# First tile in written order, with the float64 weights' last bits made by ScalarE

## The chip, the cores and the metric

One core of a Trainium2 chip runs the program. Its engines are TensorE (PE, with its weight loads PEld), VectorE (DVE), ScalarE (ACT), GpSimd (POOL) and SyncE (SP), which issues nearly all DMAs. The metric is the device time of one execution in microseconds, lower is better. An engine works through its instructions in the order in which they stand in its queue; where one waits, everything behind it on that engine waits too.

## The reference

Attention through 32 packed queries per head, then a two-dimensional Fourier transform added to its input, then a normalised two-layer network with a residual. 8 batches, 8 heads, 576 tokens, head size 64, so x has 576 rows of 512 for each batch and 4608 rows in all.

```python
def sm_attn(qq, kk, vv):
    s = scale * np.matmul(qq, kk.transpose(0, 1, 3, 2))
    s = s - np.max(s, axis=-1, keepdims=True)
    a = np.exp(s)
    a = a / (np.sum(a, axis=-1, keepdims=True) + 1e-09)
    return np.matmul(a, vv)
p_packed = sm_attn(p, k, v)
out = sm_attn(q, p_packed, p_packed)
...
X = np.fft.fft(x, axis=1)
X = np.fft.fft(X, axis=2)
mixed = np.real(X).astype(np.float32)
u = x + mixed
mu = np.mean(u, axis=-1, keepdims=True)
var = np.mean((u - mu) ** 2, axis=-1, keepdims=True)
un = (u - mu) / np.sqrt(var + 1e-06)
ch = np.maximum(un @ w_ch1, 0.0) @ w_ch2
return (u + ch).astype(np.float32)
```

The two weight matrices, 512x2048 and 2048x512, come in as float64 and are made float32 on the chip.

## The kernel before

**The work.** The 4608 rows are cut into 36 blocks of 128, and the blocks into nine tiles of four. The network (`ffn`) takes one tile at a time. Its hidden layer of 2048 is cut into 16 chunks j of 128. `up(j)` makes the hidden values of chunk j: 12 matmuls of 128x512 into the PSUM tile `ph`, of which there is one. ACT then takes `hh`, the rounded relu of `ph`, and DVE `hl`, what the rounding left. `down(j)` adds chunk j to the four sums `acc`: 12 matmuls again. Values and weights are split into a rounded part and a rest (`wr_h` by ACT, `wr_l` by POOL, line 107 inside `split`; `uh`, `ul` for the rows), and every product is three matmuls. A pair `wr_h`, `wr_l` is made anew for each chunk, matrix and tile.

**The loop.** For chunk j the program writes: `up(j)`, a split, `step(2j)`, `down(j-1)`, a split, `step(2j+1)`. Each `step` also runs one piece of the front of the next batch, the generator `front(b)`: scores `s`, exponentials, packed values `po`, spectra `pg`, `py`, `pz`, values `px`, and at the end the blocks `ubuf`. In the first tile this is the front of batch 1, and its pieces go by the letters of `ORDER[1]`; a `y` there ends a half step's piece. The letters that matter here: `e0 q1 e1` stand in step 14 and `m0`, `m1`, `a0 a1` in steps 15, 16 and 17 (softmax of the second attention for head groups 0 and 1; POOL makes the three sweeps over `s` for group 0, DVE for group 1). `f0 r0 h0` stand in step 18 and `f1 r1 h1` in step 20: they fold the transposed weights `a` into `eo` and `f` and split `f` into `fh` (ACT) and `fl` (DVE); group 0 is folded by POOL, group 1 by DVE. Still in step 20 come the products `py` and `pyr` of table t = 0 from `fh`, `fl`, `gh`, `gl` of both groups, and in step 21 those of t = 1.

**The order of the queues.** From the second tile on, PE, DVE, ACT and POOL work in the order in which the program is written (`tc.manual_schedule`). In the first tile `nullcontext()` stands there instead: a scheduler sets the order of all queues, by its own costs. SP's order is the scheduler's in all tiles.

**The weights.** The first tile runs while the weights still come in. Chunk (j, n) of matrix n is 512 KB of float64, seen as pairs of 32-bit words. It is fetched into one of the places of the `STG` tables: a negative number is a part of the weights' own final storage that isn't written yet (`w1f`, `w2f`), 9 is a part of `ubuf`, `None` one of the two `wst` tiles. Then it is converted by three instructions of 128x512: `top` (ACT) takes sign, exponent and upper digits from the high word, and `bits` (DVE) shifts that by 3 and puts in the top 3 bits of the low word. Chunks 0 and 1 are done ahead of the tile; `load_weights(j + 2)` does both chunks of j + 2 in every even step, from step 0 to step 26.

Of the kernel before, what the change touches and what calls it, by code (L numbers as in the profile page):

```python
# [1 line left out]

# [1 line left out]

# [76 lines left out]
def tile_kernel(ctx, tc, kpT, qT, v, w1, w2, tabH, tabL, tabR, tabB, tabT, sel, ident_d, out):  # L81
    nc = tc.nc
# [63 lines left out]
    fetched = {}  # L146

    def spot(n, part, shape):

        t = (w1f, w2f)[n].rearrange("p j n -> p (j n)")[:, (part % NJ) * DM:]  # L150
        size = shape[1] * shape[2]
        return t[:, 0:size].rearrange("p (a n) -> p a n", a=shape[1])

    def fetch(j, n):
        i = stages.pop(0)
        if i is None:
            st = work.tile([P, 512, 2], I32, tag="wst", name="wst", bufs=2)
        elif i < 0:
            st = spot(n, i, [P, 512, 2]).bitcast(I32)
        else:  # L160
            st = ubuf[:, i:i + 2, :].rearrange("p a n -> p (a n)").bitcast(I32).rearrange("p (n t) -> p n t", t=2)
        nc.sync.dma_start(st, (w1, w2)[n][:, j, :].bitcast(I32).rearrange("p (n t) -> p n t", t=2))
        fetched[j, n] = st

    def chunk(j, n):
        return (w1f, w2f)[n][:, j, :].bitcast(I32)

    def top(j, n):
        if (j, n) not in fetched:
# [4 lines left out]
        return nc.scalar.activation(c.bitcast(F32), high.bitcast(F32), AF.Prelu, scale=REBIAS, alpha=-2.0 ** 32)

    def bits(j, n):
        low, c = fetched.pop((j, n))[:, :, 0], chunk(j, n)
        nc.vector.tensor_scalar(c, c, 3, None, ALU.logical_shift_left)
        nc.vector.scalar_tensor_tensor(c, low, 29, c, ALU.logical_shift_right, ALU.bitwise_or)  # L179
# [7 lines left out]
    meant = {}  # L190
# [60 lines left out]
    def front(b):  # L251
# [41 lines left out]
        def scores(*gs):  # L293
# [11 lines left out]
            for g in gs:  # L305
# [101 lines left out]
        def less_one(g):  # L407
# [6 lines left out]
            def exps():  # L414
                nc.scalar.activation(s2, s2, AF.Exp, scale=0.125)
                nc.scalar.activation(s2, s2, AF.Copy, bias=-1.0)

# [105 lines left out]
        def folded_parts(g):  # L523
# [10 lines left out]
            def low():  # L534
# [94 lines left out]
        for t, base in enumerate((0, FO) if b else ()):  # L629
# [15 lines left out]
            st = work.tile([P, N2], F32R, tag=f"yr{t}", name="yr", bufs=1)  # L645
# [376 lines left out]
```

## Time and profile before

| | |
|---|---|
| device time, median of 3 | 1011.98 us (1010.78 to 1012.79) |
| the profiled execution | 1009.1 us, of it 1007.3 us span |
| ahead of the first network tile | 0 to about 50 us |
| first tile, from the first `hh` to the sixteenth | 56.5 to 170.7 us |
| second tile, the same | 180.2 to 278.4 us |
| busy over the span | PE 96%, PEld 79%, DVE 61%, POOL 46%, ACT 42% |

PE is the engine that counts: it is busy nearly all the time, so the kernel gets shorter only where PE stops waiting or has less to do. In the first tile PE has waits that the later tiles don't have. Busy time of DVE, ACT or POOL matters there only when PE waits for what they make.

### The profile page before, as it was taken

How to read it: one execution, taken by the hardware profiler on the slowest of the kernel's cores; microseconds unless marked ns; L12 is line 12 of the kernel's file. 1: busy time of each engine (PE TensorE's matmuls, PEld its weight loads, DVE VectorE, ACT ScalarE, POOL GpSimd, SP SyncE). 2: the span in 40 equal slices, each digit the busy share in tenths (PEclk: the TensorE clock that was granted, in tenths of full speed). 3: DMA queues.
4: the chain of work that ended last, by engine and by line, in shares of the span. 5: the costliest groups of instructions: out<-in, count | busy, mean ns of one | idle time of the engine just before them, and what ended most of it. 6: DMA issues, size and time to landing. Idle time of an engine off the chain costs nothing.

```text
span 1007.3 us, 15127 instructions
## 1 busy us (share of the span) xinstructions
PE 971.7 (96%) x5706; PEld 792.3 (79%) x5706; DVE 610.9 (61%) x1215; ACT 424.6 (42%) x882; POOL 465.7 (46%) x413
## 2 busy tenths in 40 slices
PE   6899799999999999999999999999999999999998
PEld 4777587878877887788878887778778888887886
DVE  5888986578555956685657755694658452323112
ACT  3466345444444445343444444443433443233322
POOL 3236625455336434553445435543454354544443
PEclk9999999999999999999999999999999999999999
DMA  9336440310122004300231114110211010111001
GB/s 352 119 110 223 151 126 22 142 50 21 43 95 98 22 1 135 99 21 22 84 102 49 43 42 142 50 63 18 99 48 37 27 63 1 47 38 43 0 1 43
DMA packets 36938, 72.82 MB, mean 72 GB/s; under 512 B 4225, under 2 KB 18433, under 8 KB 36865
## 3 DMA queue, kind: packets, MB, share of 16 engines
q1 hardware_dynamic: 35856, 70.34, 20.6%
q0 software_dynamic: 1008, 1.51, 0.5%
q8 instruction: 45, 0.74, 0.3%
q14 instruction: 29, 0.23, 0.1%
HBM read 55.58 MB, written 16.25 MB: 71 GB/s over the span
## 4 chain that ended last, share of the span: by engine, by line
PE 71%; DVE 13%; issue 7%; POOL 4%; ACT 3%; DMA 1%; ACTq 0%; SPq 0%; POOLq 0%; DVEq 0%
PE ph L789 32%; PE acc L806 27%; POOL wr_l L107 3%; DVE turned L453 1%; DVE turned L447 1%; PE po L350 1%; DVE hl L796 1%; PE s L289 1%; PE px L249 1%; PE px L247 1%; PE px L248 1%; ACT hh L795 1%; PE pz L247 1%; PE e1tp L327 1%; PE py L249 1%
## 5 line engine op out<-in xcount | busy, mean ns | idle before, releaser
L107 POOL TENSOR_TENSOR wr_l<-w1f,wr_h 128x512 fp32r<-128x512 f32 x144 | 189.4, 1317 | 393.7 <-ACT wr_h L104 392.8
L796 DVE SCALAR_TENSOR_TENSOR hl<-ph,hh 128x512 fp32r<-128x512 f32 x144 | 98.6, 685 | 298.9 <-ACT hh L795 298.7
L789 PE MATMUL ph<-uh,wr_h 128*128 128x512 f32 (+1 forms) x580 | 230.1, 397 | 10.5 <-DVE hl L796 6.6
L107 POOL TENSOR_TENSOR wr_l<-w2f,wr_h 128x512 fp32r<-128x512 f32 x144 | 195.9, 1361 | 86.0 <-ACT wr_h L104 80.2
L806 PE MATMUL acc<-wr_l,hh 128*128 128x512 f32 x576 | 225.8, 392 | 5.5 <-POOL wr_l L107 5.5
L789 PE MATMUL ph<-uh,wr_l 128*128 128x512 f32 (+1 forms) x580 | 226.3, 390 | 1.5 <-POOL wr_l L107 1.5
L806 PE MATMUL acc<-wr_h,hh 128*128 128x512 f32 x576 | 226.3, 393 | 1.2 <-ACT wr_h L104 1.2
L789 PE MATMUL ph<-ul,wr_h 128*128 128x512 f32 (+1 forms) x580 | 226.1, 390 | 0.0
L806 PE MATMUL acc<-wr_h,hl 128*128 128x512 f32 x576 | 224.9, 390 | 0.0
L795 ACT ACTIVATE hh<-ph 128x512 fp32r<-128x512 f32 x144 | 86.1, 598 | 325.7 <-PE ph L789 325.7
L789 PEld LDWEIGHTS ph<-uh,wr_h 128*128 128x128 f32 x580 | 109.3, 188 | 47.0 <-issue 15.4
L806 PEld LDWEIGHTS acc<-wr_l,hh 128*128 128x128 f32 x576 | 108.1, 188 | 29.7 <-POOL wr_l L107 9.0
L789 PEld LDWEIGHTS ph<-uh,wr_l 128*128 128x128 f32 x580 | 109.1, 188 | 25.3 <-POOL wr_l L107 2.0
L806 PEld LDWEIGHTS acc<-wr_h,hh 128*128 128x128 f32 x576 | 108.1, 188 | 24.0 <-ACT wr_h L104 2.2
L789 PEld LDWEIGHTS ph<-ul,wr_h 128*128 128x128 f32 x580 | 109.5, 189 | 21.5 <-issue 0.8
L806 PEld LDWEIGHTS acc<-wr_h,hl 128*128 128x128 f32 x576 | 108.2, 188 | 22.8
L104 ACT CAST wr_h<-w2f 128x512 fp32r<-128x512 f32 x144 | 89.4, 621 | 0.0
L104 ACT CAST wr_h<-w1f 128x512 fp32r<-128x512 f32 x144 | 88.4, 614 | 1.5 <-DVE w1f L179 1.3
L223 ACT ACTIVATE junk<-ubuf,stat 128x512 f32<-128x512 f32 x36 | 25.9, 720 | 55.9 <-DVE stat L218 55.9
L107 POOL TENSOR_TENSOR gl<-turned,gh 128x516 fp32r<-128x516 f32 x14 | 21.8, 1555 | 18.7 <-ACT gh L104 18.7
L227 POOL TENSOR_TENSOR stat<-stat,mhalf 128x1 f32<-128x1 f32 x36 | 24.6, 696 | 6.9 <-DVE stat L226 6.9
L453 DVE TENSOR_TENSOR turned<-turned 128x258 f32<-128x258 f32 x32 | 27.5, 898 | 0.5
(207 smaller groups left out, 1283.4 us busy)
## 6 DMA issues: line engine op xcount, KB each, us to landing
kp<-kpT SPq DMA_DIRECT2D x16, 608.0 KB, 5.0
out<-ubuf SPq DMA_DIRECT2D x36, 256.0 KB, 2.1
vt<-v SPq DMA_DIRECT2D x14, 640.0 KB, 4.4
wst<-w SPq DMA_DIRECT2D x17, 512.0 KB, 3.8
qt<-qT SPq DMA_DIRECT2D x14, 576.0 KB, 4.6
far<-unt SPq DMA_DIRECT2D x26, 256.0 KB, 2.0
back<-far SPq DMA_DIRECT2D x104, 64.0 KB, 2.0
ubuf<-w SPq DMA_DIRECT2D x9, 512.0 KB, 3.6
```

The lines of the kernel that those rows point to most:

```text
L104: copied = nc.scalar.copy(hi, src)
L107: (lo_eng or nc.vector).tensor_tensor(lo, src, hi.bitcast(F32), ALU.subtract)
L223: nc.scalar.activation(junk, u, AF.Square, bias=st[:, 1:2], scale=-sign, accum_out=st[:, 2:3])
L227: nc.gpsimd.tensor_tensor(st[:, 2:3], st[:, 2:3], mhalf, ALU.pow)
L247: nc.tensor.matmul(o, lh, rh, start=first, stop=False)
L248: nc.tensor.matmul(o, lh, rl, start=False, stop=False)
L249: nc.tensor.matmul(o, ll, rh, start=False, stop=last)
L453: TW[TA[min(b, 2)]].tensor_tensor(prod[0][:, t, :], prod[0][:, t, :], prod[1][:, t, :], ops[t])
L789: nc.tensor.matmul(ph[:, t], l[:, c * P:(c + 1) * P], r[:, c, t], start=(k == 0), stop=(k == 11))
L795: nc.scalar.activation(hh[:, :T], ph[:, :T], AF.Relu)
L796: nc.vector.scalar_tensor_tensor(hl[:, :T], ph[:, :T], 0.0, hh[:, :T].bitcast(F32), ALU.max, ALU.subtract)
L806: nc.tensor.matmul(acc[i], l[:, w], r, start=(j == 0 and k == 0), stop=(j == NJ - 1 and k == 2))
```

## The change

Four things, all in the first tile and just ahead of it.

1. The first tile is under `tc.manual_schedule` like the others: PE, DVE, ACT and POOL follow the written order there too.
2. A new ACT instruction `lows` reads one byte of each low word, the one with its three top bits, and writes byte/32 - 0.5 + 1/64 as an integer in the place of the low word. `bits` is then one DVE instruction, which shifts and joins, in the place of two.
3. Conversions are dealt to all half steps by the table `TAKES` (1 or 2 chunks at a time, all 28 done by step 22) instead of two in every even step until step 26.
4. Fetches follow a table `STAGES` with nine places (six parts of the weights' own storage, the part of `ubuf`, two `wst` tiles); a chunk is fetched as soon as what was in its place before has been converted (`fetch_free`). Five fetches (`W4` to `W8`) are written ahead of the tile, and so are the `lows` of the first four chunks (`u0` to `u3`).

```diff
-ORDER = ("K0 K1 V0 I0 Q0 V1 W0 Q1 B0 W1 W2 W3 i70 s0 x0 s1 i40 t0 x1 p0 b0 T0 t1 n0 w0 d0 T1 i20 v0 z0 T2 q0 e0 p1 "
...
+ORDER = ("K0 K1 V0 I0 Q0 V1 W0 Q1 B0 W1 W2 W3 i70 s0 x0 s1 i40 t0 x1 p0 b0 T0 t1 n0 w0 u0 d0 T1 i20 v0 z0 T2 W4 W5 W6 W7 W8 q0 e0 p1 "
...
-STG0 = [-2, -2, -4, -4, -6, -6]
-STG1 = [9, None, None]
+STAGES = [-2, -2, -4, -4, -6, -6, 9, 0, 1, -2, -2, -4, -4, -6, -6, 9, 0, 1, -2, -2, -4, -4, 9, 0, 1, -2, -2, 9, 0, 1, 9, 0]
+TAKES = [1, 1, 1, 2, 1, 2, 1, 2, 1, 2, 1, 2, 1, 1, 1, 1, 1, 1, 1, 1, 1, 1, 1, 1, 1, 1, 1, 1, 1, 1, 1, 1]
...
+    def fetch_free():
+
+        while line:
+            j, n = line[0]
+            i = STAGES[2 * j + n]
+            if last_in.get((i, i < 0 and n)) in fetched:
+                break
+            fetch(j, n)
...
+    def lows(j, n):
+        st = fetched[j, n]
+        byte = st.rearrange("p n t -> p (n t)").bitcast(U8).rearrange("p (n t) -> p n t", t=8)[:, :, 3]
+        return nc.scalar.activation(st[:, :, 0], byte, AF.Copy, bias=-0.5 + 1.0 / 64, scale=1.0 / 32)
 
     def bits(j, n):
         low, c = fetched.pop((j, n))[:, :, 0], chunk(j, n)
-        nc.vector.tensor_scalar(c, c, 3, None, ALU.logical_shift_left)
-        nc.vector.scalar_tensor_tensor(c, low, 29, c, ALU.logical_shift_right, ALU.bitwise_or)
-
-    def load_weights(j):
-        for n in range(2):
-            tc.keep_in_program_order(top(j, n))
+        nc.vector.scalar_tensor_tensor(c, c, 3, low, ALU.logical_shift_left, ALU.bitwise_or)
+
+    todo = [(j, n) for j in range(LEAD, NJ) for n in range(2)]
+
+    def load_weights(count):
+        for j, n in todo[:count]:
+            top(j, n)
+            lows(j, n)
             bits(j, n)
-
-
-
+            fetch_free()
+        del todo[:count]
...
-            if t == 0 and i % 2 == 0 and i // 2 + LEAD < NJ:
-                load_weights(i // 2 + LEAD)
+            if t == 0:
+                load_weights(TAKES[i])
...
-        with tc.manual_schedule(engines=MANUAL) if t > 0 else nullcontext():
+        with tc.manual_schedule(engines=MANUAL):
             ffn(first, cur, step, nxt, t + 1 >= B)
```

What it moves, at three places. Line numbers of the changed kernel are 17 to 19 higher from `bits` on.

PE in step 20 of the first tile, the products `py` and `pyr` of table 0 and `down(9)` (the `acc` rows; head group 0's products stand further up in both). Before:

```order
L806 MATMUL acc_667<-wr_h,hl 128x512
L806 MATMUL acc_668<-wr_h,hh 128x512
L247 MATMUL py<-gh,fh 128x258
L248 MATMUL py<-gl,fh 128x258
L247 MATMUL py<-gh,fh 128x258
L248 MATMUL py<-gl,fh 128x258
L247 MATMUL pyr<-gh,fh 101x258
L248 MATMUL pyr<-gl,fh 101x258
L806 MATMUL acc_668<-wr_l,hh 128x512
L249 MATMUL py<-gh,fl 128x258 x2
L249 MATMUL pyr<-gh,fl 101x258
L806 MATMUL acc_668<-wr_h,hl 128x512
```

The same place now:

```order
L266 MATMUL py<-gh,fh 128x258
L267 MATMUL py<-gl,fh 128x258
L268 MATMUL py<-gh,fl 128x258
L266 MATMUL pyr<-gh,fh 101x258
L267 MATMUL pyr<-gl,fh 101x258
L268 MATMUL pyr<-gh,fl 101x258
L266 MATMUL pyr<-gh,fh 101x258
L267 MATMUL pyr<-gl,fh 101x258
L268 MATMUL pyr<-gh,fl 101x258
L825 MATMUL acc_674<-wr_h,hh 128x512
L825 MATMUL acc_674<-wr_l,hh 128x512
L825 MATMUL acc_674<-wr_h,hl 128x512
```

Group 1's products stood behind ten of the twelve matmuls of `down(9)`; now all eighteen products of both groups stand ahead of all twelve. In the same way the fourteen `pz` products of batch 0, which stood in between the transposes ahead of and inside `up(0)`, now stand behind `up(0)`.

DVE from `hl` of chunk 8 to that of chunk 9 (`s`, `z`, `d`, `a` are the second softmax; L179, then L196, and L178 are the conversions). Before, from the first of the two on:

```order
L796 SCALAR_TENSOR_TENSOR hl<-ph,hh 128x512
L427 RECIPROCAL z_1328<-z_1328 128x18
L178 TENSOR_SCALAR w1f<-w1f 128x512
L465 TENSOR_TENSOR s_1265<-s_1265,z_1328 128x576
L179 SCALAR_TENSOR_TENSOR w1f<-wst,w1f 128x512
L178 TENSOR_SCALAR w2f<-w2f 128x512
L467 STREAM_TRANSPOSE a<-s_1265 128x576
L179 SCALAR_TENSOR_TENSOR w2f<-ubuf,w2f 128x512
L511 MEMSET f 128x3x2
L530 SCALAR_TENSOR_TENSOR xl<-eo,xh 128x256
L498 TENSOR_TENSOR f<-eo 128x2x3x15
```

The same place now, with both `hl`:

```order
L815 SCALAR_TENSOR_TENSOR hl<-ph,hh 128x512
L443 TENSOR_REDUCE z_1354<-s_1290 128x18
L444 TENSOR_SCALAR d_1355<-z_1354 128x18
L445 TENSOR_SCALAR z_1354<-z_1354 128x18
L446 RECIPROCAL z_1354<-z_1354 128x18
L447 TENSOR_TENSOR s_1290<-s_1290,d_1355 128x576
L196 SCALAR_TENSOR_TENSOR w2f<-w2f 128x512
L486 STREAM_TRANSPOSE a<-s_1136 128x576
L484 TENSOR_TENSOR s_1290<-s_1290,z_1354 128x576
L486 STREAM_TRANSPOSE a<-s_1290 128x576
L196 SCALAR_TENSOR_TENSOR w1f<-w1f 128x512
L815 SCALAR_TENSOR_TENSOR hl<-ph,hh 128x512
```

The softmax of both groups stands later against the chunks than it did (group 0's transposed `a` was made one chunk earlier before), and the next `hl` stands behind ten instructions, two of them conversions.

ACT from `hh` of chunk 9 to that of chunk 10 (`w1f` and `w2f` rows are conversions by `top`, rows that write `ubuf` or `wst` are `lows`). Before:

```order
L795 ACTIVATE hh<-ph 128x512
L104 CAST wr_h<-w1f 128x512
L521 CAST fh<-f 128x776
L174 ACTIVATE w1f<-wst 128x512
L174 ACTIVATE w2f<-wst 128x512
L104 CAST wr_h<-w2f 128x512
L515 ACTIVATE xh<-eo 128x256
L517 CAST oh<-eo 128x256
L795 ACTIVATE hh<-ph 128x512
```

The same place now:

```order
L814 ACTIVATE hh<-ph 128x512
L105 CAST wr_h<-w1f 128x512
L534 ACTIVATE xh<-eo 128x256
L536 CAST oh<-eo 128x256
L540 CAST fh<-f 128x776
L187 ACTIVATE w2f<-ubuf 128x512
L192 ACTIVATE ubuf<-ubuf 128x512
L105 CAST wr_h<-w2f 128x512
L187 ACTIVATE w1f<-wst 128x512
L192 ACTIVATE wst<-wst 128x512
L814 ACTIVATE hh<-ph 128x512
```

Before, the `xh` and `oh` in this piece were group 1's; now they are group 0's, and `hh` of chunk 10 stands behind `fh` of group 0, two conversions of two instructions each and a split.

More of the change, by code (lines that the diff above doesn't have):

```diff
@@ L1 @@
-from contextlib import ExitStack, nullcontext
+from contextlib import ExitStack
 import numpy as np
@@ L12 @@
 I32 = mybir.dt.int32
+U8 = mybir.dt.uint8
 AF = mybir.ActivationFunctionType
@@ L37 @@
 TL = (0, 0, 0)
-ORDER = ("K0 K1 V0 I0 Q0 V1 W0 Q1 B0 W1 W2 W3 i70 s0 x0 s1 i40 t0 x1 p0 b0 T0 t1 n0 w0 d0 T1 i20 v0 z0 T2 q0 e0 p1 "
-         "b1 i80 l0 d1 w1 w2 w3 m0 q1 a0 e1 g0 i122 f0 r0 F0 l1 m1 n1 g1 i203 a1 j0 h0 J0 H0 P0 f1 r1 i64 j1 F1 h1 J1 X0 "
+ORDER = ("K0 K1 V0 I0 Q0 V1 W0 Q1 B0 W1 W2 W3 i70 s0 x0 s1 i40 t0 x1 p0 b0 T0 t1 n0 w0 u0 d0 T1 i20 v0 z0 T2 W4 W5 W6 W7 W8 q0 e0 p1 "
+         "b1 i80 l0 d1 w1 w2 w3 m0 q1 a0 e1 g0 i122 f0 r0 F0 l1 m1 n1 g1 i203 a1 j0 h0 J0 H0 P0 f1 r1 i64 j1 F1 u1 u2 u3 h1 J1 X0 "
          "H1 P1",
@@ L123, in tile_kernel @@
     idles = [psf.tile([P, 512], F32, tag="ph", name="idle")]
-    stages = (STG0 + STG1 * 40)[:2 * NJ]
     tbh = [cpool.tile([P, KT], F32R, name=f"tbh{t}") for t in range(2)]
@@ L152, in spot @@
         return t[:, 0:size].rearrange("p (a n) -> p a n", a=shape[1])
+    line = [(j, n) for j in range(NJ) for n in range(2)]
+    last_in = {}
     def fetch(j, n):
-        i = stages.pop(0)
-        if i is None:
+        assert line.pop(0) == (j, n)
+        i = STAGES[2 * j + n]
+        assert last_in.get((i, i < 0 and n)) not in fetched
+        last_in[i, i < 0 and n] = j, n
+        if i < 0:
+            st = spot(n, i, [P, 512, 2]).bitcast(I32)
+        elif i < 2:
             st = work.tile([P, 512, 2], I32, tag="wst", name="wst", bufs=2)
-        elif i < 0:
-            st = spot(n, i, [P, 512, 2]).bitcast(I32)
         else:
@@ L163, in fetch @@
         fetched[j, n] = st
+    def fetch_free():
+        while line:
+            j, n = line[0]
+            i = STAGES[2 * j + n]
+            if last_in.get((i, i < 0 and n)) in fetched:
+                break
+            fetch(j, n)
     def chunk(j, n):
@@ L168, in top @@
     def top(j, n):
-        if (j, n) not in fetched:
-            fetch(j, n)
         high, c = fetched[j, n][:, :, 1], chunk(j, n)
         return nc.scalar.activation(c.bitcast(F32), high.bitcast(F32), AF.Prelu, scale=REBIAS, alpha=-2.0 ** 32)
+    def lows(j, n):
+        st = fetched[j, n]
+        byte = st.rearrange("p n t -> p (n t)").bitcast(U8).rearrange("p (n t) -> p n t", t=8)[:, :, 3]
+        return nc.scalar.activation(st[:, :, 0], byte, AF.Copy, bias=-0.5 + 1.0 / 64, scale=1.0 / 32)
     def bits(j, n):
         low, c = fetched.pop((j, n))[:, :, 0], chunk(j, n)
-        nc.vector.tensor_scalar(c, c, 3, None, ALU.logical_shift_left)
-        nc.vector.scalar_tensor_tensor(c, low, 29, c, ALU.logical_shift_right, ALU.bitwise_or)
-    def load_weights(j):
-        for n in range(2):
-            tc.keep_in_program_order(top(j, n))
+        nc.vector.scalar_tensor_tensor(c, c, 3, low, ALU.logical_shift_left, ALU.bitwise_or)
[4 more added lines that the diff above has]
+            lows(j, n)
             bits(j, n)
+            fetch_free()
+        del todo[:count]
     u_of, stat_of, place_of, free = {}, {}, {}, list(range(NU))
@@ L545, in front @@
                  "W": lambda i: fetch(i // 2, i % 2), "w": lambda i: top(i // 2, i % 2),
-                 "v": lambda i: bits(i // 2, i % 2),
+                 "v": lambda i: bits(i // 2, i % 2), "u": lambda i: lows(i // 2, i % 2),
                  "F": folded_high, "z": lambda _: next(splits)}
```

## The prediction

> **What bounds the kernel now.** I read the share of busy time first, then busy time by stretch, then PE's waits in the first tile, then that stretch engine by engine. Busy us, share of the span and instructions of each engine:
>
> ```profile
> PE 971.7 (96%) x5706; PEld 792.3 (79%) x5706; DVE 610.9 (61%) x1215; ACT 424.6 (42%) x882; POOL 465.7 (46%) x413
> ```
>
> PE bounds the whole; DVE, the next that makes what PE waits for, has 61%. Now busy time by engine in three windows: a part of the first tile, its rest, and the second tile. After each engine's name stand its busy us, at the end the granted clock and the DMA load.
>
> ```profile
> 104.00:137.00 33.00, 25.43 (x121) 19.36 (x121) 30.72 (x63) 14.84 (x28) 16.90 (x13) 0.95 0.47 146
> 137.00:171.00 34.00, 33.27 (x177) 27.89 (x176) 24.81 (x52) 17.18 (x39) 15.03 (x13) 1.00 0.27 79
> 178.00:279.00 101.00, 100.61 (x622) 83.03 (x621) 66.33 (x136) 43.51 (x94) 45.37 (x38) 1.00 0.18 61
> ```
>
> In the second tile PE is busy 100.6 of 101 us: nothing is to be had there, and the diff does not touch it. In the first tile PE stands still almost only from 104 to 137 us, where DVE is busy 30.7 of 33 us. These are PE's waits in the first tile, with total, times and longest in us:
>
> ```profile
> PE ph L789 <- DVE hl L796: 6.2, 2, 3.2
> PE ph L789 <- POOL wr_l L107: 1.5, 1, 1.5
> PE acc L806 <- ACT wr_h L104: 1.2, 1, 1.2
> PE py L247 <- ACT fh L521: 0.9, 1, 0.9
> PE acc L806 <- POOL wr_l L107: 0.7, 1, 0.7
> PE s2T L289 <- DVE turned L447: 0.5, 1, 0.5
> ```
>
> Together 11.0 us. Of these 1.5 and 1.2 lie ahead of the end of `up(7)`, the 0.5 right behind it, 6.2 are the waits for `hl` of chunks 8 and 9, 0.9 is the wait of group 1's `py` for `fh`, and 0.7 comes late in the tile. The long waits have a second price, PE's clock behind the second of them (window, PE busy, clock):
>
> ```profile
> 123.00:126.00 3.00, 0.29 (x2) 1.00 0.67 198
> 126.00:129.40 3.40, 3.09 (x7) 0.50 0.00 0
> ```
>
> Half clock for 3.4 us is 1.7 us lost. So 12.7 us is all that can be won. The conversions' part in it, by group (count, busy us, mean ns):
>
> ```profile
> L178 DVE TENSOR_SCALAR w2f<-w2f 128x512 int32<-128x512 int32 x16 | 13.8, 865 | 0.2 <-ACT w2f L174 0.2
> L178 DVE TENSOR_SCALAR w1f<-w1f 128x512 int32<-128x512 int32 x14 | 9.6, 689 | 3.8 <-ACT w1f L174 3.6
> L179 DVE SCALAR_TENSOR_TENSOR w2f<-wst,w2f 128x512 int32<-128x512 int32 x9 | 10.8, 1196 | 0.1
> ```
>
> [...]
>
> ```profile
> 114.87 1.29 POOL L107 TENSOR_TENSOR wr_l<-w1f,wr_h 128x512 fp32r<-128x512 f32 x1 [3.46 <-ACT wr_h L104]
> 114.94 1.25 DVE L426 TENSOR_SCALAR z<-z 128x18 f32<-128x18 f32 x1
> 117.89 1.84 POOL L107 TENSOR_TENSOR wr_l<-w2f,wr_h 128x512 fp32r<-128x512 f32 x1 [1.73 <-ACT wr_h L104]
> 118.49 1.79 DVE L179 SCALAR_TENSOR_TENSOR w1f<-wst,w1f 128x512 int32<-128x512 int32 x1
> 121.73 0.65 DVE L179 SCALAR_TENSOR_TENSOR w2f<-ubuf,w2f 128x512 int32<-128x512 int32 x1
> ```
>
> A shift of 18 numbers took 1.25 us and ended with POOL's `wr_l`; a conversion that started 0.6 us into another `wr_l` took 1.79 us, and one that met no POOL instruction 0.65 us. [...]
>
> **The change part by part.** All times are of the one profiled execution, 1009.1 us with its span of 1007.3; the median of the runs is 2.9 us above it.
>
> Ahead of the tile: ACT gets one `lows` at 13 us and three at 41 us. A neighbouring ACT conversion starts 0.57 us behind the one before it:
>
> ```profile
> 83.44 0.67 ACT L174 ACTIVATE w1f<-ubuf 128x512 f32<-128x512 f32 x1
> 84.01 0.65 ACT L174 ACTIVATE w2f<-wst 128x512 f32<-128x512 f32 x1
> ```
>
> No row has a byte as input or integers as output, so 0.57 is an estimate from these; its lower end is 0.5, its upper end I put at 1.0 for a rival below. Three at 41 us stand where ACT idles before `yh`, the one at 13 us replaces DVE's shift there: counted at nothing, cover gone it is 0.2 us. The fetches written earlier were issued ahead of the tile by the scheduler too, all but two, and a conversion comes 10 us and more after its fetch can start: nothing.
>
> Waits ahead of `up(7)`. With written order and one DVE instruction less for each chunk I count for chunks 0 to 6, instruction by instruction, ACT at most 6.6 us a chunk (three conversions 3.4, `hh` and two `wr_h` 1.5, the front 1 to 1.7) against 6.2 to 6.8 of PE, and `hl` ready 2 us before the next `up` needs its bank. The two waits go: -2.7 us. Against that the fourteen `pz` products filled waits inside `up(0)` and now stand in PE's line, each 0.12 us:
>
> ```profile
> 138.61 0.28 PE L247 MATMUL py<-gh,fh 128*128 128x258 f32 x1
> 138.73 0.28 PE L248 MATMUL py<-gl,fh 128*128 128x258 f32 x1
> ```
>
> 14 x 0.12 = +1.7 us.
>
> From the end of `up(7)` to the end of `down(9)`. Before, it runs from `hh` of chunk 7 to the first matmul behind `down(9)`, with the end of `up(10)` in it:
>
> ```profile
> 104.25 0.60 ACT L795 ACTIVATE hh<-ph 128x512 fp32r<-128x512 f32 x1 [0.27 <-PE ph L789]
> 130.79 0.60 ACT L795 ACTIVATE hh<-ph 128x512 fp32r<-128x512 f32 x1 [1.25 <-PE ph L789]
> 136.75 0.40 PE L789 MATMUL ph<-uh,wr_h 128*128 128x512 f32 x1
> ```
>
> 32.5 us: 26.5 to the end of `up(10)` and 6.0 more. The 26.5 hold waits of 0.5, 3.2 and 3.0 and 1.7 of half clock, so PE's work is 18.1.
>
> Now the first part. The softmax of both groups starts in step 14. ACT's exponentials wait for POOL's sweep over group 0, which stands behind `wr_l`, `gl` and has 1.16 us itself; then four of them hold ACT 2.6 us, then a conversion, then comes `hh(8)`: its `hl` is ready about 0.6 us after PE wants the bank. Between `hl(8)` and `hl(9)` DVE has ten instructions:
>
> ```profile
> L412 POOL TENSOR_TENSOR s<-s,m 128x576 f32<-128x576 f32 x1 | 1.2, 1161 | 0.4 <-DVE m L411 0.4
> L415 ACT ACTIVATE s<-s 128x576 f32<-128x576 f32 x2 | 1.4, 688 | 2.4 <-DVE s L412 2.4
> 113.95 0.75 DVE L424 TENSOR_REDUCE z<-s 128x18 f32<-128x576 f32 x1
> 116.11 0.75 DVE L428 TENSOR_TENSOR s<-s,d 128x576 f32<-128x576 f32 x1
> 121.03 0.77 DVE L467 STREAM_TRANSPOSE a<-s 128x576 f32<-128x576 f32 x1
> ```
>
> Reduction 0.75, three short ones 0.65, three sweeps and transposes at 0.75 plus one more, two conversions 0.65 each and `hl` 0.68 make 6.4 us, against 5.4 of PE (`up(9)`, `down(8)`, 24 matmuls at 0.23). Six of the ten can meet a POOL instruction (`wr_l` three times, a sweep, `eo`). With no meeting PE waits 2 us over the two chunks, with every meeting 6; I take 4, between, since the rows above met in most cases but POOL is not always busy. So 22.1 us, with 20.1 and 24.1 as ends, 4 us earlier than before.
>
> Second part, from the end of `up(10)`. The order now puts all of `py` ahead of `down(9)`, and group 1's `py` needs its `fl`. What must still happen, in each queue's order:
>
> ```profile
> 132.80 0.75 DVE L498 TENSOR_TENSOR f<-eo 128x90 f32<-128x90 f32 x1
> 133.94 0.17 DVE L513 TENSOR_SCALAR f<-a 128x31 f32<-128x31 f32 x1
> 134.15 0.84 ACT L521 CAST fh<-f 128x776 fp32r<-128x776 f32 x1 [2.25 <-DVE f L513]
> 126.58 0.45 DVE L480 TENSOR_TENSOR eo<-a 128x287 f32<-128x287 f32 x1
> 135.02 0.97 DVE L536 TENSOR_TENSOR fl<-f,fh 128x776 fp32r<-128x776 f32 x1 [0.58 <-ACT fh L521]
> 82.23 0.39 PE L806 MATMUL acc<-wr_h,hh 128*128 128x512 f32 x1
> ```
>
> POOL's folding of group 0 ends about when `up(10)` does. Then the rest of the folding on DVE 1.3 (132.80 to 134.11), `fh` of group 0 0.85, on ACT two conversions and a `wr_h` that stand ahead of `hh(10)` 2.8, `hh` 0.6, `hl` 0.7, group 1's four folds 1.5 (the first took 0.45 with its start), the rest 1.3, `fh` 0.85, `fl` 0.95, the last thirteen products 1.6, `down(9)` 2.7: 15.1 us, with meetings of DVE and POOL 15.6. Before it was 6.0, since ten matmuls of `down(9)` and group 0's products filled PE's time until `fl` came. Queued behind the waiting `py` now are `down(9)`, `py` of table 1 and `up(11)`.
>
> Together 37.2 us, ends 35.2 and 39.7: +4.7 us, from +2.7 to +7.2.
>
> The clock. PE stands still for some 10 us in the second part. The rows have half clock for 3.4 us after a wait of 3.0 us, and none after one of 3.2 us, so the cost lies between 0 and 1.7 us; I take 1.5, since this wait is three times as long. [...] No run here shows so long a wait.
>
> After `down(9)`. The conversions end at step 22 instead of 26, and the late wait goes: -0.7 us. The turn to the second tile is the same code: nothing.
>
> Sum: -2.7 + 1.7 + 4.7 + 1.5 - 0.7 = +4.5 us. That is 1013.6 us for a profiled execution and 1016.5 us against the median of 1012.
>
> **The rivals.** *Faster, because DVE is relieved.* In the stretch from 104 to 137 us DVE loses six shifts and half of its meetings with POOL. If group 1's `fl` came as soon as `up(10)` is done, the second part would be 4.9 us and the gain 2.7 - 1.7 + (32.5 - 20.1 - 4.9) + 0.7 = 9.2 us, 1003 us. For it speaks DVE's 93%; against it that `hh(10)`, `hl(10)` and group 1's folding all stand behind `fh` of group 0 in their queues. It decides when `fl` ends less than 28 us after `up(7)` (by my count it is 32 to 35): then the whole is faster by 2 us or more, 1008 to 1010.
>
> *No change.* Meetings at their lower end and no half clock: -2.7 + 1.7 + 2.7 - 0.7 = +1.0 us, 1013.
>
> *ScalarE becomes the bound.* If `lows` takes 1.0 us, each chunk with three conversions gets 1.3 us more, 8 us of ACT against 6.4 of PE; over chunks 1 to 5 PE waits some 5 us more for `hh`: 1021.5. ACT's 14.8 busy us of 33 speak against it for the tile as a whole, the front-loaded table for it at its start.
>
> **How the numbers follow.** The written order's wait at `py` (forecast) 0.51, ACT as the bound 0.06, no change 0.20, faster 0.23. 0.2% is 2.0 us, about what a measurement of this kernel can tell. So faster 0.23, same 0.20, slower 0.57. The forecast's own range is 1014 to 1019. The range to hold eight in ten goes down to 1007, into the faster case, and up to 1021.5 for ACT and a second half clock.
>
> **What would show it.** Right: in the changed profile PE has one wait of 8 to 11 us at a `py` product for `fh` or `fl`, about 25 us behind the seventh chunk, and half clock behind it; waits of 1 to 4 us for `hl` before `up(9)` and `up(10)`; none of note before `up(7)`, which ends 1.5 us earlier; DVE's conversions at 28 x 0.65 to 1.2 us; `lows` near 0.6 us. Wrong: a short wait at `py`, then the chain of group 1 was quicker than I put together; or waits for `hh` from chunk 1 on, then ACT is the bound; or a DMA as a releaser, then a place came free too late.

## The result and the profile after

1016.09 us median of 5 runs (1014.8 to 1017.91) against 1010.78 us for the kernel before on the same chip: ratio 1.0053, 95% interval 1.0041 to 1.0066. The prediction was 1016.5 us, slower. The profiled execution took 1014.8 us, its span 1013.0.

Engine totals (the page's busy times), and the same three windows as before:

```profile
PE 974.5 (96%) x5706; PEld 795.4 (79%) x5706; DVE 589.1 (58%) x1183; ACT 442.1 (44%) x914; POOL 463.1 (46%) x413
```

```profile
104.00:137.00 33.00, 22.29 (x98) 16.11 (x97) 29.37 (x60) 19.65 (x36) 19.71 (x16) 0.86 0.33 99
137.00:171.00 34.00, 34.00 (x174) 29.57 (x174) 13.95 (x36) 16.16 (x37) 11.25 (x12) 0.93 0.00 1
178.00:279.00 101.00, 100.62 (x624) 82.70 (x624) 66.80 (x133) 44.06 (x93) 45.86 (x38) 1.00 0.17 59
```

DVE's 610.9 us became 589.1, ACT's 424.6 became 442.1, as the diff says. From 104 to 137 us PE has less busy time than before (22.3 us against 25.4), at a lower clock (0.86 against 0.95); the second tile is the same. PE's waits in the first tile, with total, times and longest (0.6 us of the first row, 0.5 of the fourth and the last row lie ahead of the first `hh`, as do 1.9 us for `un` that are not shown):

```profile
PE py L266 <- ACT fh L540: 6.9, 2, 6.3
PE ph L808 <- DVE hl L815: 4.1, 2, 2.9
PE s L308 <- ACT e L335: 2.7, 1, 2.7
PE py L268 <- DVE fl L555: 0.7, 2, 0.5
PE ph L808 <- ACT uh L105: 0.7, 1, 0.7
```

The long ones as PE's own rows (in brackets the idle time ahead, and what ended it):

```profile
61.41 1.06 PE L308 MATMUL s<-kp 64*32 64x512 f32 x8 [2.70 <-ACT e L335]
115.67 0.47 PE L808 MATMUL ph<-uh,wr_h 128*128 128x512 f32 x1 [1.18 <-DVE hl L815]
124.39 0.53 PE L808 MATMUL ph<-uh,wr_h 128*128 128x512 f32 x1 [2.91 <-DVE hl L815]
135.62 0.58 PE L266 MATMUL py<-gh,fh 128*128 128x258 f32 x1 [6.30 <-ACT fh L540]
```

From this the tile can be laid beside the one before, by the starts of ACT's `hh` (`hh` of chunk 0, 7 and 15, then the first of the second tile: 55.96, 104.75, 176.41 and 185.81 in the changed kernel; the end of `down(9)` is 143.35):

| part | before | after | difference | forecast |
|---|---|---|---|---|
| ahead of the first `hh` | 56.50 | 55.96 | -0.5 | 0 |
| to `hh` of chunk 7 | 47.75 | 48.79 | +1.0 | -1.0 |
| to the end of `down(9)` | 32.50 | 38.60 | +6.1 | +6.2 (4.7 and 1.5) |
| to `hh` of chunk 15 | 33.98 | 33.06 | -0.9 | -0.7 |
| to the second tile | 9.42 | 9.40 | 0 | 0 |

The sum is +5.7, the difference of the two profiled executions. So the loss sits where it was forecast, between `up(7)` and `down(9)`. The chain that ends in the 6.3 us, from three engines' rows in order of time:

```profile
124.31 0.74 POOL L502 TENSOR_TENSOR f<-eo 128x256 f32<-128x256 f32 x1
126.13 0.84 ACT L540 CAST fh<-f 128x776 fp32r<-128x776 f32 x1 [2.60 <-DVE f L532]
128.52 0.68 ACT L187 ACTIVATE w1f<-wst 128x512 f32<-128x512 f32 x1
129.09 0.66 ACT L192 ACTIVATE wst<-wst 128x512 int32<-128x512 uint8 x1
129.63 0.59 ACT L814 ACTIVATE hh<-ph 128x512 fp32r<-128x512 f32 x1
130.46 0.68 DVE L815 SCALAR_TENSOR_TENSOR hl<-ph,hh 128x512 fp32r<-128x512 f32 x1
131.06 1.35 DVE L499 TENSOR_TENSOR eo<-a 128x287 f32<-128x287 f32 x1
134.72 0.84 ACT L540 CAST fh<-f 128x776 fp32r<-128x776 f32 x1 [1.51 <-DVE f L532]
135.60 0.97 DVE L555 TENSOR_TENSOR fl<-f,fh 128x776 fp32r<-128x776 f32 x1 [0.24 <-ACT fh L540]
```

`up(10)` was done at 128.9. ACT takes `hh(10)` at 129.6, behind group 0's `fh` and the conversions; DVE starts group 1's folding (`eo`, 131.06) only behind `hl(10)`; `fh` of group 1 follows at 134.7 and releases PE. ACT's `hh(10)` has no bracket: the engine came from another instruction and did not wait.

### The profile page after: what moved, and what is told of

Its sections match the earlier page's. It is cut to its first block, busy times and chain, and to the rows that moved or that the text cites. A ratio compares the mean times of both kernels' runs of the same rounds, so it can differ in the third digit from the quotient of the medians.

```text
span 1013.0 us, 15129 instructions
## 1 busy us (share of the span) xinstructions
PE 974.5 (96%) x5706; PEld 795.4 (79%) x5706; DVE 589.1 (58%) x1183; ACT 442.1 (44%) x914; POOL 463.1 (46%) x413
## 4 chain that ended last, share of the span: by engine, by line
PE 73%; DVE 10%; issue 7%; POOL 4%; ACT 4%; DMA 2%; SPq 0%; ACTq 0%; POOLq 0%; DVEq 0%
PE ph L808 33%; PE acc L825 28%; POOL wr_l L108 3%; DVE turned L472 1%; PE po L369 1%; DVE turned L466 1%; PE px L268 1%; PE px L266 1%; PE px L267 1%; DMA w1f<-w 1%; PE py L268 1%; DVE hl L815 1%; PE pz L266 1%; PE pz L267 1%; PE pz L268 1%
## 5 line engine op out<-in xcount | busy, mean ns | idle before, releaser
L108 POOL TENSOR_TENSOR wr_l<-w2f,wr_h 128x512 fp32r<-128x512 f32 x144 | 193.5, 1344 | 85.0 <-ACT wr_h L105 83.9
L108 DVE TENSOR_TENSOR yl<-py,yh 128x258 fp32r<-128x258 f32 x32 | 13.6, 426 | 23.7 <-ACT yh L105 23.0
L684 DVE SCALAR_TENSOR_TENSOR ubuf<-qe,pe 128x512 f32<-128x512 f32 x32 | 26.8, 873 | 0.6
```

The costliest lines, as they stand in the source:

```text
L108: (lo_eng or nc.vector).tensor_tensor(lo, src, hi.bitcast(F32), ALU.subtract)
L684: nc.vector.scalar_tensor_tensor(u_of[key], qe, sign, pe, ALU.mult, ALU.add, accum_out=stat_of[key][:, 0:1])
```

## The experiments

All are compared with runs of the kernel before on the same chip. Tile is the time from the first `hh` to the first `hh` of the second tile in the profiled execution: 123.7 us before, 129.9 after.

| run | edit | ratio to before (95%) | tile, us |
|---|---|---|---|
| the change | | 1.0053 (1.0041 to 1.0066) | 129.9 |
| e1_fold | after, folding a half step earlier | 1.0008 (0.9998 to 1.0017) | 125.3 |
| e2_fill | after, `py` repeated in the wait | 1.0054 (1.0038 to 1.0070) | 131.9 |
| e3_gap | after, no conversions in steps 14 to 18 | 1.0045 (1.0028 to 1.0062) | 127.6 |
| e4_s1 | after, scores of group 1 in step 3 | 1.0043 (1.0031 to 1.0055) | 129.7 |
| e5_sched | after, scheduler's order | 1.0050 (1.0036 to 1.0064) | 118.7 |
| e6_written | before, written order alone | 1.0117 (1.0104 to 1.0130) | 137.6 |
| e7_lows0 | after without `lows` | 1.0111 (1.0096 to 1.0125) | 136.2 |
| e8_apart | after, `ORDER[1]` and `TAKES` rearranged | 0.9972 (0.9960 to 0.9984) | 122.5 |
| e9_sched_pin | e5 with ACT's conversions pinned | 0.9980 (0.9970 to 0.9989) | 123.9 |
| e10_apart_s1 | e8 and e4 together | 0.9961 (0.9948 to 0.9974) | 120.5 |
| e11_mixed | e10 with 8 `lows` fewer | 0.9964 (0.9952 to 0.9976) | 119.7 |

Theory 1: the written order is the loss, since group 1's folding stands behind `hh(10)` and `hl(10)`. Its rivals: `lows` are the loss, because they load ACT; or the amount of work between `up(7)` and `down(9)` sets the time, whatever its order.

### Which part of the change costs: e6, e7, e5, e9

e6 is the kernel before with `nullcontext()` taken away:

```diff
-        with tc.manual_schedule(engines=MANUAL) if t > 0 else nullcontext():
+        with tc.manual_schedule(engines=MANUAL):
```

> The kernel before with the first part of the change alone: the first tile in written order, conversions as before (two in each even step, two DVE instructions each, no lows). Theory 1, the written order is the loss and lows with the dealt conversions give a part of it back: the same wait at py of 6 us or more, longer waits for hl, since DVE has 23 us more to do: 1018 to 1022 us, 1.007 to 1.011 of before. Rival, lows are the loss: about as before, 1009 to 1013 us.

Measured 1.0117, just over theory 1's range; its first three waits:

```profile
PE py L247 <- ACT fh L521: 8.8, 3, 7.9
PE s L289 <- ACT e L316: 3.7, 1, 3.7
PE ph L789 <- DVE hl L796: 2.9, 2, 1.9
```

The wait at `py` and the one at the scores are there without any `lows`: they belong to the written order.

e7 keeps everything but `lows`:

```diff
-            lows(j, n)
-            bits(j, n)
+            bits2(j, n)
```

`bits2` is the pair from before the change: one DVE instruction shifts the word by 3, a second puts in the top 3 bits of the low word.

> The changed kernel without lows in the first tile: its 28 conversions there are again two DVE instructions and no ACT one; written order, TAKES and places stay. Theory 1, DVE's relief is worth something in the stretch from up(7) to down(9), where 8 conversions stand: each shift costs 0.4 to 1.2 us there, hl of chunks 8 and 9 comes 2 to 4 us later, and half clock may follow: 1018 to 1021 us. Rival, what lows take from ACT (0.57 us each, and two of them ahead of hh(10)) counts as much as they give DVE: 1014 to 1017 us. If ACT is the bound in chunks 2 to 7, these get shorter and the wait at the scores near 61 us, which stands behind a lows, shrinks: up(7) ends 1 to 2 us sooner.

Measured 1.0111, just over theory 1's range (1.0111 times 1010.8 is 1022). PE's waits for `fh` and `hl`, against 6.9 and 4.1 us with `lows`:

```profile
PE py L270 <- ACT fh L544: 10.6, 3, 7.9
PE ph L812 <- DVE hl L819: 4.9, 2, 3.7
```

`lows` win 5.8 thousandths of the time, some 6 us. What lies between e6 and e7, the conversions dealt to half steps and the nine places, cannot be told from nothing (1.0117 and 1.0111). The third expectation missed: the scores still wait 2.6 us, for with DVE's shift it took 1.79 us from the start of the tile's first `top` to the first maximum (58.47 to 60.26 us in e7), and 1.88 us with `lows` (57.92 to 59.80).

e5 and e9 undo the written order and keep the rest:

```diff
-        with tc.manual_schedule(engines=MANUAL):
+        with tc.manual_schedule(engines=MANUAL) if t > 0 else nullcontext():
```

> The changed kernel with its first part alone undone: the scheduler orders the first tile again (nullcontext), while lows, the one-instruction bits, TAKES and the nine places stay. Theory 1, the written order is the loss: PE's waits at the scores (2.7 us) and at py (6.3 us) go, DVE has 28 shifts less than before the change: 1005 to 1009 us, 0.994 to 0.998 of before. Rival, ScalarE: ACT has no idle time between two hh from 66 to 105 us in the changed kernel because of lows; if that is the bound, the scheduler's order does not help and PE waits for hh or wr_h in chunks 2 to 7: 1012 us or more.

1.0050, a miss of the total. The tile is 118.7 us, 5.0 shorter than before, but it begins 9.2 us later. ACT's first `un`, which the blocks of the tile come from, in the changed kernel and in e5:

```profile
48.02 1.34 ACT L890 ACTIVATE un<-ubuf,stat 128x512 f32<-128x512 f32 x2 [1.60 <-DVE stat L237]
```

```profile
54.77 1.32 ACT L890 ACTIVATE un<-ubuf,stat 128x512 f32<-128x512 f32 x2
```

Right ahead of it, from 47 us on, ACT works through nine conversion instructions of the tile (five `top`, four `lows`) that the scheduler drew forward; with those further up it is 25 (13 and 12), nearly half of the tile's 56. Before the change `top` was pinned to the program's order, and e5 had lost that pin. e9 puts it back:

```diff
-            top(j, n)
-            lows(j, n)
+            tc.keep_in_program_order(top(j, n))
+            tc.keep_in_program_order(lows(j, n))
```

> As e5 (the scheduler orders the first tile of the changed kernel), but top and lows keep their place in the program's order, as top did before the change. In e5 the scheduler had put 8 conversions on ACT ahead of the blocks' un, and the first hh came at 65.7 us in place of 56.0. Theory 1, the written order is the loss: the first hh comes at 56 to 57 us again and the tile takes e5's 118.7 us from there: 1005 us, 0.994 of before. Rival, ScalarE's lows: what was won in e5's tile was only that conversions had been done ahead of it; with them back in the tile it takes 124 us or more, 1011 us and up.

0.9980: faster than before, with the longest wait at `py` 2.2 us, but not the 0.994 of theory 1. The tile is 123.9 us in this execution, so most of e5's short tile was work done ahead of it; that part of the rival holds. Still the four corners stand clear: without `lows` 1 and 1.011 (scheduler, written order), with them 0.998 and 1.005. The written order costs 11 to 12 us without `lows` and 7 with them; `lows` win 6 us in the written order, and with the new dealing 2 us in the scheduler's.

### What the wait at py is made of: e1, e3, e2

e1 moves the front one half step ahead from the spectra on, and group 1's folding right behind group 0's:

```diff
- ... q0 d1 y y g0 y g1 y ... a0 a1 y f0 r0 h0 y y f1 r1 h1
+ ... q0 d1 y g0 y g1 y ... a0 a1 y f0 r0 h0 y f1 r1 h1 y y
```

> The changed kernel (1016.1 us, 1.0053 of before) with one edit to ORDER[1]: everything from the spectra of the packed values to the folding stands one half step earlier, and group 1 is folded in the half step right behind group 0; the products py stay in step 20. Nothing is added or removed. Theory 1, the order of the queues: PE's wait of 6.3 us at py came because group 1's folding stood behind hh(10) and hl(10). It goes, with the 2.1 us of half clock behind it: 1008 us, 0.997 of before; PE waits under 1 us at py. Rival, the amount of work: DVE, ACT and POOL have the same to do between up(7) and down(9), so the wait only moves to hl of chunks 8 to 10: 1013 to 1016 us.

1.0008, between the two. The wait of 6.3 us is gone, and from `hh` of chunk 7 to that of chunk 11 the time falls from 43.7 to 36.4 us: 7.3 of the 8 us expected. The rival has a part too: one wait of 4.1 us ahead of `up(10)`, with its reason in ACT's row:

```profile
130.32 0.77 PE L808 MATMUL ph<-uh,wr_h 128*128 128x512 f32 x1 [4.13 <-DVE hl L815]
126.89 0.84 ACT L540 CAST fh<-f 128x776 fp32r<-128x776 f32 x1 [2.60 <-DVE f L532]
128.75 0.58 ACT L814 ACTIVATE hh<-ph 128x512 fp32r<-128x512 f32 x1
```

`hh(9)` stands behind `fh` of group 0, which waited 2.6 us for the folding. So a part of the wait moved to the next value that stands behind `fh`; most of it did not. In this execution 4.4 us of the 7.3 were lost again ahead of `hh(7)`, which starts at 109.19 us instead of 104.75: the clock was 0.51 at the tile's start, from 50 to 57 us (last section), and from `hh(5)` to `hh(7)`, where the moved spectra now stand, it took 1.2 us more.

e3 takes the conversions out of the crowded steps:

```diff
-TAKES = [..., 1, 2, 1, 1, 1, 1, 1, 1, 1, 1, 1, 1, 1, 1, ...]   # steps 10 to 23
+TAKES = [..., 1, 2, 1, 1, 0, 0, 0, 0, 0, 2, 1, 1, 2, 2, ...]
```

> The changed kernel with TAKES alone edited: no conversion in steps 14 to 18 (there was one in each), they follow in steps 19 to 24. Theory 1, conversions meet POOL instructions: the five conversions at 1.0 to 1.8 us in the stretch, with top and lows on ACT, are what makes hl late: PE's waits for hl of 1.2 and 2.9 us and the 1.6 us of half clock behind them go, and fh of group 1 comes 1 to 2 us sooner: 1009 us, 0.998 of before. Rival, the softmax alone fills DVE: sweeps, reductions and transposes keep hl late: 1013 to 1015 us, PE's waits for hl still 3 us together. A third: the conversions moved to steps 19 to 24 stand ahead of group 1's folding there and make the wait at py longer: over 1016 us.

```profile
PE py L266 <- ACT fh L540: 9.3, 3, 7.2
PE ph L808 <- DVE hl L815: 0.5, 1, 0.5
```

The mechanism came as theory 1 says, 4.1 us of waits for `hl` became 0.5; the time did not: the waits for `fh` grew from 6.9 to 9.3 us, and 1.0045 cannot be told from 1.0053. An earlier `up(10)` only waits longer for group 1's chain. What conversions meet on POOL is seen again in the changed kernel: one that began 0.6 us into POOL's `wr_l` took 1.78 us; the same operation 18 us later, which began with POOL at rest, took 0.69 us:

```profile
109.84 1.81 POOL L108 TENSOR_TENSOR wr_l<-w2f,wr_h 128x512 fp32r<-128x512 f32 x1
110.41 1.78 DVE L196 SCALAR_TENSOR_TENSOR w2f<-w2f,wst 128x512 int32<-128x512 int32 x1
128.14 0.69 DVE L196 SCALAR_TENSOR_TENSOR w2f<-w2f,ubuf 128x512 int32<-128x512 int32 x1 [0.17 <-ACT ubuf L192]
```

e2 fills the wait with repeated products, to price the clock alone:

```diff
+                    for _ in range(16 if b == 1 and t + c + g == 0 else 0):
+                        three(py[:, :N2], fh[g][:, w], fl[g][:, w], gh[g][:, t, :], gl[g][:, t, :], True, True)
```

> The changed kernel with sixteen repetitions of the first three py products of group 0 in step 20, 48 matmuls of 0.12 us = 5.8 us, in the wait of 6.3 us at group 1's py; each repetition overwrites the same sums, so the values stay. It measures the clock term alone. Theory 1: the half clock at 135.6 to 141.7 us comes from PE standing still: the wait is 0.5 us long now, the clock stays at 1.0 and the 2.1 us come back: 1014 us, 1.003 of before. Rival: the half clock has another cause (or the wait isn't the path): 1016 us, with clock 0.5 still in the records. If the added matmuls run at half clock after the wait before up(10), they take longer than the wait and the time is 1016 or more.

1.0054: nothing won. PE busy time, clock (third column from the end) in the changed kernel behind its waits of 2.9 and 6.3 us, and in e2 behind the wait of 2.9 us ahead of `up(10)` and behind what is left at `py`, 1.3 and 0.5 us:

```profile
124.40:127.70 3.30, 3.30 (x9) 2.59 (x10) 2.28 (x12) 1.57 (x3) 0.65 (x1) 0.54 0.01 2
136.00:141.60 5.60, 5.40 (x20) 4.71 (x20) 2.11 (x5) 2.53 (x6) 0.00 (x0) 0.50 0.01 3
```

```profile
128.60:138.60 10.00, 9.53 (x63) 8.69 (x63) 7.65 (x23) 5.38 (x10) 3.33 (x3) 1.00 0.33 108
140.90:143.90 3.00, 3.00 (x14) 3.00 (x15) 0.85 (x2) 0.75 (x2) 0.00 (x0) 0.50 0.00 0
```

In e2 `up(10)` ran at full clock (1.00) behind a wait of 2.9 us; behind one of the same length the changed kernel had 0.54, and e2 itself had 0.50 for 3 us behind 1.3 and 0.5 us. From chunk 7 to 11 the time fell by 0.9 us, from 43.7 to 42.8. So in these rows half clock comes behind waits, but not behind each, and the length of the last wait alone does not tell which; the price of 2.1 us for this place isn't confirmed, 0.9 was measured in one execution, and the median shows none.

### The unforeseen wait: e4, e10, e11

Why PE waits at 61.4 us, by DVE and ACT of the changed kernel:

```profile
58.52 0.64 ACT L192 ACTIVATE w1f<-w1f 128x512 int32<-128x512 uint8 x1
59.19 0.69 DVE L196 SCALAR_TENSOR_TENSOR w1f<-w1f 128x512 int32<-128x512 int32 x1 [1.91 <-ACT w1f L192]
59.93 0.68 DVE L327 TENSOR_REDUCE mx<-s 128x1 f32<-128x512 f32 x1
60.95 0.31 ACT L335 ACTIVATE e<-s1t,nb 128x64 f32<-128x64 f32 x1 [1.80 <-DVE nb L329]
```

The first conversion of the tile stands ahead of the maxima of the scores in DVE's queue, and it waited for `lows`; the exponentials (`e`) wait for the maxima, and the scores of group 1 for the exponentials. The scores had been there since 58.7 and the first maximum started at 59.8, so some 1.1 of the 2.7 us are the conversion's; the rest is the time of the maxima and exponentials, during which the written order gives PE nothing else to do. e4 puts those scores behind `up(1)`:

```diff
- s0 s1 y y t0 ...
+ s0 y s1 y t0 ...
```

> The changed kernel with one edit to ORDER[1]: the scores of group 1 stand in step 3 instead of step 1. It tells what the unforeseen wait of 2.7 us at 61.4 us is worth: PE waits there for ACT's exponentials of group 0, which wait for DVE's maxima, which stand behind a conversion that waits for lows. Theory 1: the wait was on the path; with up(1) ahead of these scores 2 to 3 us come back: 1013.5 us, 1.003 of before. Rival: up(1) then waits for something else at the same place, or the later scores delay e1T and packed values: 1016 us.

1.0043, not to be told from 1.0053. The wait is gone and `hh(1)` comes 2.6 us sooner after the first `hh` (7.1 us against 9.7), but by `hh(7)` that is lost: 48.6 us against 48.8. Where it goes:

```profile
69.18 0.32 ACT L335 ACTIVATE e<-s1t,nb 128x64 f32<-128x64 f32 x1 [3.14 <-DVE nb L329]
72.36 0.58 ACT L814 ACTIVATE hh<-ph 128x512 fp32r<-128x512 f32 x1
73.99 0.30 PE L349 MATMUL e1tq<-ident,e 128*64 128x128 f32 x1 [0.79 <-ACT e1T L352]
```

`up(2)` was done at 69.5, but `hh(2)` starts at 72.36, without a bracket: ACT stood still for 3.1 us until the maxima of group 1 came, and then had their exponentials and four conversion instructions ahead of `hh(2)`. At the end of `up(2)` PE is 2.4 us ahead of the changed kernel, at the end of `up(3)`, behind the wait of 0.8 us, only 1.1. e8 takes the long waits away first, with one place for each piece:

```diff
- ... p0 y y y d0 p1 y q0 d1 y y g0 y g1 y ... a0 a1 y f0 r0 h0 y y f1 r1 h1
+ ... p0 y y d0 p1 y q0 d1 y g0 y g1 y ... a0 a1 y f0 y r0 h0 y f1 r1 h1 y y
-TAKES = [..., 1, 2, 1, 1, 1, 1, 1, 1, 1, 1, 1, 1, 1, 1, 1, ...]   # steps 10 to 24
+TAKES = [..., 1, 2, 0, 0, 0, 0, 0, 0, 0, 2, 1, 2, 2, 2, 2, ...]
```

> The changed kernel with ORDER[1] and TAKES edited for PE's waits: the softmax of step 14 starts in step 12 (two empty half steps are taken out), group 0's sums f0 stand in step 16, its rest r0 h0 in step 17, group 1's folding in step 18, py stays in step 20; no conversion in steps 12 to 18, they follow in steps 19 to 24. Theory 1, the waits for hl and py are made by what stands ahead of them in the queues: hl of chunks 8 to 10 waits under 1 us in all, py under 1.5 us, no half clock in the stretch, which takes 28 us in place of 38.6: 1005 us, 0.995 of before. Rival, the moved pieces find the same conflicts earlier: waits of 2 to 4 us for hl of chunks 7 and 8: 1009 us, or the fetches come too late behind the gap (a DMA as the releaser from chunk 12 on): 1012 us.

0.9972: faster than both. The window that was worst, and the waits:

```profile
104.00:137.00 33.00, 28.07 (x127) 21.30 (x126) 24.70 (x55) 16.49 (x32) 20.13 (x18) 1.00 0.15 50
```

```profile
PE s L308 <- ACT e L335: 2.7, 1, 2.7
PE acc L825 <- POOL wr_l L108: 2.3, 2, 1.6
PE ph L808 <- DVE hl L815: 1.2, 2, 0.6
PE py L266 <- ACT fh L540: 1.2, 2, 0.6
```

PE has 28.1 busy us in the window instead of 22.3, the clock is full, and PE waits for no fetch. The waits in the tile are 1.2 us for `hl`, where theory 1 has under 1, and 1.1 at `py`, where it has under 1.5 (0.6 for `fh`, since the other 0.6 of the row lie ahead of the tile, and 0.5 for `fl`); `wr_l` took 2.3 us, which was not expected. From `hh(7)` to `hh(11)` it takes 30.3 us instead of 43.7. The time is 1008.5, not 1005: the first seven chunks took 54.7 us instead of 48.8, since part of the moved work stands there now; 1.4 of these lie ahead of `hh(1)`, with half clock in them (0.51 from 63 to 66 us). e10 is e8 with e4's edit:

```diff
- s0 s1 y y t0 ...
+ s0 y s1 y t0 ...
```

> e8 (0.9972 of before) with the scores of group 1 in step 3 in place of step 1, the edit of e4. Theory, ScalarE is the bound in chunks 2 to 7, where ACT goes from one hh to the next without a pause: the wait of 2.7 us at the scores goes, and what it saves is lost again by up(7), as in e4: 1008 to 1009 us, 0.997. Rival, e4's gain was hidden by the long waits behind it and shows now that these are gone: 1006 us.

0.9961, nearer the rival; its interval overlaps that of e8, so that this 1 us is not shown. Its tile is 2.0 us shorter. e11 gives eight conversions back to DVE:

```diff
-            lows(j, n)
-            bits(j, n)
+            if n and j < 10:
+                bits2(j, n)
+            else:
+                lows(j, n)
+                bits(j, n)
```

> e10 with the second weight's conversions up to chunk 9 made by two DVE instructions in place of lows and one: 8 lows or 4.6 us less on ACT in chunks 1 to 7, 8 shifts more on DVE, which has idle time there. Theory, ScalarE is the bound in chunks 2 to 7: now the 2 to 3 us of the earlier scores stay won: 1005 to 1006 us, 0.995 of before. Rival, DVE's shifts meet POOL's wr_l and make hl late: 1008 us or more.

e11 gained nothing over e10 (0.9964), although ACT's busy time between 64 and 104 us fell from 32.3 to 29.3 us, shown here for the changed kernel, e10 and e11:

```profile
64.00:104.00 40.00, 40.00 (x272) 31.86 (x271) 25.72 (x49) 34.86 (x70) 21.54 (x21) 1.00 0.69 231
```

```profile
64.00:104.00 40.00, 38.91 (x280) 28.22 (x279) 28.29 (x57) 32.29 (x67) 21.86 (x21) 1.00 0.72 240
```

```profile
64.00:104.00 40.00, 38.73 (x280) 28.18 (x279) 32.99 (x63) 29.27 (x61) 21.80 (x20) 1.00 0.74 247
```

So the theory that ScalarE is the bound in chunks 2 to 7 isn't borne out: 3 us less on ACT left PE's 38.9 busy us as they were, and in the changed kernel ACT has 5 idle us of these 40, while PE has none. PE's own work sets the pace there, and e10 and e11 could win at most the 1.1 to 1.3 us in which it stood still. e7 says the same: without any `lows` it took 39.15 us from `hh(1)` to `hh(7)`, against 39.11 in the changed kernel.

## Why the prediction was right, step by step

- **The stretch from `up(7)` to `down(9)`**: forecast 37.2 us and 1.5 of half clock, measured 38.6. The mechanism is shown: e1 takes 7.3 us away by moving pieces of the front and nothing else, e6 brings the wait without the other parts. Inside the stretch the two halves were mis-sized against each other. To the end of `up(10)` it took 24.2 us against 22.1, at the forecast's upper end of 24.1: the waits for `hl` were 1.2 and 2.9 us, together the 4 us forecast, but 3.3 us at about half clock fell there too, and `up(10)` took 4.4 us where it takes 2.8 in e2. From there to the end of `down(9)` it took 14.4 us against 15.1 and the clock's 1.5. The step that failed is "POOL's folding of group 0 ends about when `up(10)` does": it ended at 125.05, 3.8 us sooner, so `fh` of group 0 was out of the way, and the wait at `py` was 6.3 us instead of 8 to 11. More half clock took a part of that back: the last thirteen products and `down(9)`, from 136.62 us on, took 6.7 us against 4.3 and the clock's 1.5. That the stretch as a whole came within 0.1 us is luck.
- **Ahead of `up(7)`**: forecast -1.0, measured +1.0. The two waits went as forecast (-2.7), and the fourteen `pz` products stand in PE's line from 55.76 to 57.45 us, the 1.7 us forecast. The step that failed is the count of chunks 0 to 6 "instruction by instruction": it left out that in the written order `up(1)` stands behind the scores of group 1, and these behind the maxima and exponentials of group 0, with the tile's first conversion, which waits for ACT, ahead of the maxima (with `lows` as without, by e7). That was a wait of 2.7 us, and "none of note before `up(7)`" was wrong.
- **The clock**: half clock behind the wait at `py` came (5.6 us at 0.50 in the window above), and also behind the 2.9 us (3.3 us at 0.54). The 1.5 us in the sum was the author's estimate from two waits before the change, 3.0 us with half clock behind it and 3.2 us without. e2 shows that half clock cannot be priced from the last wait alone: 2.9 us of waiting had full clock behind it, and 1.8 us of standing still within 2.3 us had 0.50. It shows too that the first stretch of half clock cost nothing: there `up(10)` ran at full clock, and from `hh(7)` to `hh(10)` it took 24.9 us all the same, since `hh(10)` waits its turn on ACT. What decides whether half clock follows a wait was not shown.
- **`lows`**: forecast 0.57 us behind one another, and they are: 103.61, 104.18 and 104.75 are the starts of `top`, `lows` and `hh` in ACT's queue. Of the tile's 28 conversions on DVE 18 took under 0.7 us; the other ten, at 0.76 to 1.8 us, began while a POOL instruction ran. Six of the 18 overlap one too, but one that began after them; so does the prediction's conversion of 0.65 us at 121.73 us, during which POOL's `f` began at 121.95. Between `hl(8)` and `hl(9)` two sweeps and two conversions grew in this way to 5.6 us together, against 2.8 at the forecast's times without a meeting. But not every DVE instruction grew beside POOL: over the whole span the 144 `hl` took 0.65 to 0.69 us, the 16 reductions to `z` 0.73 to 0.75 and the 16 transposes to `a` 0.77 to 0.78, here a reduction inside POOL's `wr_l` of 114.84 to 116.14 us. The second line is one group of `lows`, with count, sum and mean:

```profile
115.45 0.73 DVE L443 TENSOR_REDUCE z<-s 128x18 f32<-128x576 f32 x1
L192 ACT ACTIVATE wst<-wst 128x512 int32<-128x512 uint8 x9 | 6.1, 674 | 0.0
```

- **The rivals**: "faster" fell at the place given for it. Its condition was that `fl` ends less than 28 us after `up(7)`; it ended 32.0 us after it (136.57 less 104.6). ACT as the bound did not come true: ACT was busy for 34.9 of 40 us in chunks 2 to 7, but PE for all 40, and e7 and e11 speak against it too.
- **The sum**: forecast +4.5 us, measured +5.7 between the profiled executions; 2.0 too little ahead of `hh(7)`, the other parts within 0.5 and together 0.8 too much. That the median was met within 0.4 us is partly luck: the runs of the kernel before lay 1.2 us lower this time.

## What to carry to other kernels

A written order makes each engine wait for the one thing that its author put next, as PE did for 6.3 us at `py` with `down(9)` behind it; before a scheduler's order is replaced, list what stands in the queue behind each value that another engine makes late, here `hh`, `hl` and a folding behind `fh`. Relieving an engine pays where it is waited for (6 us of `lows` in the written order, 2 us in the scheduler's, the new dealing included), and taking one wait away pays only up to the next chain: judge pieces and conversions together, as e8 does, not one by one. When an experiment undoes one part, see what else the old part had held, like the pin that e5 lost.

## What was not expected of the hardware

The same instructions with nearly the same waits at the tile's start (1.36 and 0.68 us in the changed kernel, 1.35 and 0.68 in e1) ran at full clock in one execution and at half in another. In seven traces with the written order and the scores in step 1 PE waits 2.6 to 3.7 us for them; in four of these (e1, e2, e6, e8) a low clock follows (0.62, 0.50, 0.50 and 0.51 from 63 to 66 us), in three (the change, e3, e7) it does not (1.00 in the same window). e1 has the changed kernel's order up to step 10, and yet, from 50 to 57 us, clock and busy time:

```profile
50.00:57.00 7.00, 5.78 (x44) 5.15 (x44) 6.73 (x14) 4.74 (x10) 1.30 (x1) 1.00 0.26 78
```

```profile
50.00:57.00 7.00, 6.39 (x29) 6.10 (x30) 5.94 (x11) 3.23 (x6) 1.29 (x1) 0.51 0.24 76
```

It may be a good part of why runs of one kernel differ by 3 to 6 us (e2: 1013.3 to 1019.3); that is not shown. It is a reason to conclude nothing from differences under 2 us between two single traces.
